# One unit's sums moved to an output bank pair, and stage 0's work re-ordered, in a convolution + gated-MLP kernel

## The chip, the cores and the metric

The kernel runs on one core of one Trainium2 chip. The metric is the device time of one execution in microseconds (us). All executions in this document are of mean granted TensorE clock 0.999 or 1.0 of full speed. A program on one core cannot be compared with a neighbouring core, so small differences rest on repeated runs.

## The reference

The input `x` has 8 sequences of 4096 tokens with 192 features. Each feature is convolved along its sequence with 7 taps (softmaxed weights, one set per head of 24 features). Then each of the 32768 tokens goes through a two-layer network:

```python
h = x @ w_in                                   # 192 -> 2048
g = h * (1.0 / (1.0 + np.exp(-beta * h)))      # beta: one number per hidden feature
return (g @ w_out).astype(np.float32)          # 2048 -> 192
```

## The kernel before

The kernel works in 32 **stages** of 1024 tokens (one chunk of 512 tokens from each half of the batch). A stage has 16 **units**; a unit is one block of 128 hidden features. In a unit, TensorE (PE) computes the *sums* `h` (6 matmuls into a `ph` bank pair of PSUM, 0.64 us), ScalarE applies the gate (1.1 us per unit), and PE issues some *output pairs*: two matmuls that add one hidden block's part of `g @ w_out` for 128 tokens (0.083 us per pair). An output **job** is 256 tokens x 16 blocks = 32 pairs, so a stage owes 4 jobs = 128 pairs. There are only two places for jobs, the bank pairs `pa` and `pb`; jobs alternate between them, and before a place can be used again VectorE must reduce it to SBUF.

```python
LAG = 2
def ready(self, s, u):                       # a job may use a block only LAG units after its sums
    fcs = NF if self.s < s else max(0, u - LAG + 1)
    return self.done < fcs * self.nb         # nb = 2: two pairs per block
...
def output(s, u, pairs, free):
    for _ in range(pairs):
        for name in free:
            if slots[name] is None and waiting:
                slots[name] = waiting.popleft()
        ...                                  # the oldest job that is ready issues one pair
        if job.po is None:
            job.po = place[name]()           # takes bank pair "a" or "b": PE waits here for its last reduce
        if job.pair():
            job.leave()                      # VectorE reduces, the DMA stores
            slots[name] = None
```

The main loop decides how many pairs each unit issues. Stage 0 issues fewer, because nothing older is waiting:

```python
first_work = {                               # VectorE, stage 0; None = next convolution tap of chunk 1
    4: [None, None],
    5: [None],
    6: [conv1_evac, lambda: scale_w_out(2), None],
    7: [None, lambda: rows_of(2)],
    8: [lambda: scale_w_out(3), None],
    9: [None],
}
QUOTA_A = {4: 2, 7: 4, 8: 4}
for s in range(N_ST):
    jobs_of(s)
    for u in range(NF):
        ...
        hidden(s, u)                         # the sums and their activation (cut: units 0 and 1, second())
        if s > 0:
            output(s, u, 8 if s < N_ST - 1 else 6, "ab")
        elif u > 8:
            output(s, u, 5 if u < NF - 1 else 10, "ab")
        elif u in QUOTA_A:
            output(s, u, QUOTA_A[u], "a")
        ...
```

So stage 0 issues 2 + 4 + 4 + 6 x 5 + 10 = 50 pairs, and every later stage but the last issues 16 x 8 = 128, as many as it owes.

`w_out` is multiplied by 1/beta in four quarters, the first two on GpSimd, the others on VectorE; `x` of chunk 1 is transposed on PE by a plain matmul with the identity, half of it into `pb` and half into `pa`.

## Time and profile before

| | before |
|---|---|
| median of 3 runs | 690.08 us (689.89 to 690.16) |
| span of the profiled run | 688.0 us |
| PE busy | 682.2 us, 99% |
| ScalarE / VectorE busy | 579.0 / 524.7 us |
| stage 1 starts (first sums) | 29.39 us |
| period from the start of stage 1 to that of stage 31 | 20.92 us |

The page's busy line (engine, busy us, share of the span, instructions) and the first line of the chain that ended last:

```profile
PE 682.2 (99%) x11312; PEld 521.1 (76%) x11312; DVE 524.7 (76%) x467; ACT 579.0 (84%) x530; POOL 9.9 (1%) x20
...
PE 98%; DMA 1%; ACT 0%; DVE 0%; issue 0%; ACTq 0%
```

PE bounds the kernel: it is nearly always busy and nearly the whole chain is its own work. The timeline of PE (start us, duration us, engine, line, operation, out<-in, count, and in brackets the idle time before it with what ended it) lists only two gaps after the start-up:

```profile
12.77 0.36 PE L368 MATMUL pa<-ident_b,x1b 64*128 64x64 bf16 x12
13.82 0.82 PE L424 MATMUL ph<-ct,w_in_s 64*128 64x512 bf16 x6 [0.70 <-ACT g L432]
14.82 0.82 PE L424 MATMUL ph<-ct,w_in_s 64*128 64x512 bf16 x6 [0.18 <-ACT g L432]
```

After the transposes, PE idles 0.70 us and then 0.18 us until ScalarE has freed a `ph` pair. The change aims at these. The timeline of VectorE in stage 0 (from the first tap of chunk 1) and GpSimd's second scaling:

```profile
15.39 1.69 DVE L338 TENSOR_SCALAR ct<-xt,cw 128x1024 bf16<-128x1024 bf16 x1
17.12 2.60 DVE L340 SCALAR_TENSOR_TENSOR ct<-xt,cw,ct 128x1024 bf16<-128x1024 bf16 x2
...
22.03 2.60 DVE L340 SCALAR_TENSOR_TENSOR ct<-xt,cw,ct 128x1024 bf16<-128x1024 bf16 x2
24.54 1.27 DVE L106 CAST xb<-xf 128x768 bf16<-128x768 f32 x2
...
25.81 0.94 DVE L314 TENSOR_TENSOR w_out_s<-w_out_raw,beta_r 128x768 bf16<-128x768 f32 x1
26.67 2.59 DVE L340 SCALAR_TENSOR_TENSOR ct<-xt,cw,ct 128x1024 bf16<-128x1024 bf16 x2
```

```profile
15.14 1.66 POOL L314 TENSOR_TENSOR w_out_s<-w_out_raw,beta_r 128x768 bf16<-128x768 f32 x1 [0.99 <-DMA w_out_raw<-in_moe_w_out_dram]
```

The first tap (15.39) took 1.69 us, as GpSimd's scaling ran until 16.80. The last w_out scaling (25.81) is done at 26.75; PE first needs that quarter at 27.50.

### The profile page before, as it was taken

The page shows a single profiled execution, that of the slowest core. Times are in us where ns is not written, and L with a number is a line of the kernel's source. Part 1 is how long each engine was busy: PE and PEld are TensorE (multiplying, and loading weights), DVE is VectorE, ACT ScalarE, POOL GpSimd, SP SyncE. Part 2 cuts the span into 40 slices and gives each one's busy share as a digit, 9 for nine tenths or more (in the row PEclk, how much of TensorE's full clock was granted, in tenths as well). Part 3 has the DMA queues.
Part 4 walks back from the last instruction along what each step waited for, and adds up shares of the span by engine and source line. Part 5 has one row for each costly group of instructions (what it writes and reads, how often), then busy time and mean ns, then how long its engine had stood idle before and what let it go on. Part 6 is the DMA issues. An engine that isn't in the chain of part 4 may idle for free.

```text
span 688.0 us, 24344 instructions
## 1 busy us (share of the span) xinstructions
PE 682.2 (99%) x11312; PEld 521.1 (76%) x11312; DVE 524.7 (76%) x467; ACT 579.0 (84%) x530; POOL 9.9 (1%) x20
## 2 busy tenths in 40 slices
PE   8999999999999999999999999999999999999998
PEld 4777777777777777777777777777777777777777
DVE  7989877788777787777797777887777977777712
ACT  7988888888888888888888888888888888888893
POOL 5000000000000000000000000000000000000000
PEclk9999999999999999999999999999999999999999
DMA  9734333244332244332444332444323443322111
GB/s 234 190 97 117 105 100 98 58 107 117 101 99 77 77 116 116 95 99 61 98 117 105 93 97 57 116 117 96 103 60 93 117 109 96 100 59 59 49 36 59
DMA packets 121861, 67.06 MB, mean 97 GB/s; under 512 B 53264, under 2 KB 121760, under 8 KB 121760
## 3 DMA queue, kind: packets, MB, share of 16 engines
q1 hardware_dynamic: 120048, 64.12, 34.7%
q0 software_dynamic: 1664, 1.38, 1.2%
q8 instruction: 88, 1.44, 0.9%
q14 instruction: 13, 0.11, 0.0%
q10 hardware_dynamic: 48, 0.01, 0.0%
HBM read 29.89 MB, written 25.17 MB: 80 GB/s over the span
## 4 chain that ended last, share of the span: by engine, by line
PE 98%; DMA 1%; ACT 0%; DVE 0%; issue 0%; ACTq 0%
PE ph L424 48%; PE pa L457 25%; PE pb L457 24%; DMA x<-in_x_dram 1%; PE pb L287 1%; ACT g L432 0%; PE ph L287 0%; DVE x0b L226 0%; ACT xt L302 0%; PE pa L287 0%; PE pb L233 0%; PE ph L233 0%; DVE diag L260 0%; ACT osb L473 0%; ACT beta L309 0%
## 5 line engine op out<-in xcount | busy, mean ns | idle before, releaser
L432 ACT ACTIVATE g<-ph,beta 128x1024 bf16<-128x1024 f32 x512 | 569.7, 1115 | 94.5 <-PE ph L424 89.8
L457 PEld LDWEIGHTS <-g 64*128 64x128 bf16 x8160 | 370.7, 94 | 102.3 <-issue 0.2
L424 PE MATMUL ph<-ct,w_in_s 64*128 64x512 bf16 x3072 | 424.3, 376 | 0.9 <-ACT g L432 0.9
L340 DVE SCALAR_TENSOR_TENSOR ct<-xt,cw,ct 128x1536 bf16<-128x1536 bf16 (+2 forms) x190 | 336.9, 1773 | 2.5
L457 PE MATMUL pa<-w_out_s,g 64*128 64x192 bf16 x4112 | 244.8, 243 | 0.0
L457 PE MATMUL pb<-w_out_s,g 64*128 64x192 bf16 (+1 forms) x4048 | 230.4, 243 | 0.0
L424 PEld LDWEIGHTS <-w_in_s 64*128 64x128 bf16 x3072 | 159.6, 94 | 54.8 <-issue 2.7
L475 DVE TENSOR_REDUCE osb<-pa 128x384 f32<-128x768 f32 x64 | 61.3, 958 | 122.5 <-PE pa L457 121.1
L475 DVE TENSOR_REDUCE osb<-pb 128x384 f32<-128x768 f32 x63 | 60.3, 957 | 29.1 <-PE pb L457 29.1
L106 DVE CAST xb<-xf 128x768 bf16<-128x768 f32 x60 | 40.5, 677 | 0.0
L338 DVE TENSOR_SCALAR ct<-xt,cw 128x1536 bf16<-128x1536 bf16 (+2 forms) x32 | 32.4, 1011 | 0.0
L473 ACT COPY osb<-pb 128x192 f32<-128x192 f32 x1 | 0.3, 319 | 7.2 <-PE pb L457 7.2
L211 POOL DMA_DIRECT2D w_in_s<-in_moe_w_in_dram x8 | 5.2, 662 | 0.0
L223 PE MATMUL ph<-zeros 128*128 128x512 bf16 (+2 forms) x11 | 4.1, 485 | 1.1 <-DVE warm L180 1.1
L287 PE MATMUL pb<-xt,diag 64*128 64x512 f32 (+1 forms) x21 | 4.7, 443 | 0.0
L121 DVE COPY xt<-xt 128x18 bf16<-128x18 bf16 x27 | 4.4, 164 | 0.0
L287 PEld LDWEIGHTS pb<-xt,diag 64*128 64x128 f32 (+1 forms) x21 | 2.7, 187 | 0.9 <-issue 0.4
L314 POOL TENSOR_TENSOR w_out_s<-w_out_raw,beta_r 128x768 bf16<-128x768 f32 x2 | 3.1, 1564 | 4.1 <-DVE beta_r L354 3.2
L223 PEld LDWEIGHTS <-zeros 128*128 128x128 bf16 x11 | 1.2, 121 | 2.2 <-issue 1.1
L181 ACT ACT_TABLE_LOAD x1 | 1.3, 1283 | 1.8 <-PEq L593 1.8
L226 ACT CAST x1b<-x 128x384 bf16<-128x384 f32 x3 | 2.0, 714 | 0.4 <-DMA x<-in_x_dram 0.4
L287 PE MATMUL ph<-xt,diag 128*128 128x512 f32 x7 | 1.9, 409 | 0.1
(55 smaller groups left out, 26.9 us busy)
## 6 DMA issues: line engine op xcount, KB each, us to landing
out_dram<-osb SPq DMA_DIRECT2D x127, 192.0 KB, 2.2
xf<-in_x_dram SPq DMA_DIRECT2D x60, 384.0 KB, 4.3
xt<-xb SPq DMA_TRANSPOSE x120, 2.6
x<-in_x_dram SPq DMA_DIRECT2D x4, 384.0 KB, 4.9
w_out_raw<-in_moe_w_out_dram SPq DMA_DIRECT2D x4, 384.0 KB, 13.5
w_in_s<-in_moe_w_in_dram POOLq DMA_DIRECT2D x6, 192.0 KB, 10.5
w_in_raw<-in_moe_w_in_dram SPq DMA_DIRECT2D x2, 192.0 KB, 5.6
w_in_s<-in_moe_w_in_dram POOLq DMA_DIRECT2D x2, 96.0 KB, 7.4
```

Source lines behind the costliest of these rows:

```text
L106: nc.vector.tensor_copy(xbs[ch][:, :, :, h, :], xfs[ch][:, h].rearrange("q b (p c) -> q b c p", c=NG),)
L121: nc.vector.tensor_copy(dst, last[:, :, HALO + TOK - PAD :])
L211: nc.gpsimd.dma_start(out=w_in_s[r * DG : (r + 1) * DG, :, c0:c1], in_=w_in_v[:, :, c0:c1])
L223: nc.tensor.matmul(pf[:, 0, 0:cols], zeros, zc, start=True, stop=True)
L287: nc.tensor.matmul(pv, diag[rows, k, :], xt[rows, o : o + TOK], start=(k == k0), stop=(k == K - 1),)
L314: (nc.vector if i > 1 else nc.gpsimd).tensor_tensor(w_out_s[:, fcs, :], w_out_raw[:, fcs, :], beta_r[:, fcs].unsqueeze(2).to_broadcast((12 ...
L338: nc.vector.tensor_scalar_mul(dst, src, scalar)
L340: nc.vector.scalar_tensor_tensor(out=dst, in0=src, scalar=scalar, in1=dst, op0=ALU.mult, op1=ALU.add)
L424: nc.tensor.matmul(ph[:, h, :], w_in_s[rows, j, fc * 128 : (fc + 1) * 128], cts[s][rows, j, :], start=(j == 0), stop=(j == NG - 1),)
L432: nc.scalar.activation(gs[s][:, fc], ph, AF.Silu, scale=beta[:, fc : fc + 1])
L457: nc.tensor.matmul(self.po[:, r, b * D : (b + 1) * D], g[rows, fc, self.h, q * BLK : (q + 1) * BLK], w_out_s[rows, fc, :], start=(self.don ...
L475: nc.vector.tensor_reduce(dst, self.po[:, :, 0 : nb * D].rearrange("p r n -> p n r"), axis=mybir.AxisListType.X, op=ALU.add,)
```

## The change

The intent: unit 2 need not wait for a `ph` pair if its sums go to the output pair `pa`, idle at that time. For this all of chunk 1's transposes must fit in `pb`, which they do as bf16 transposes. The convolution taps on PE are done in two units instead of three, a third scaling goes to GpSimd, VectorE's work is re-ordered, and the time won is used to issue 14 early output pairs (5 + 5 + 4) instead of 10.

```diff
--- before.py
+++ after.py
@@ -311,7 +311,7 @@
 
     def scale_w_out(i):
         fcs = slice(i * NQ, (i + 1) * NQ)
-        (nc.vector if i > 1 else nc.gpsimd).tensor_tensor(
+        (nc.vector if i > 2 else nc.gpsimd).tensor_tensor(
             w_out_s[:, fcs, :],
             w_out_raw[:, fcs, :],
             beta_r[:, fcs].unsqueeze(2).to_broadcast((128, NQ, D)),
@@ -352,39 +352,40 @@
     nc.vector.tensor_tensor(dst, pv, dst, ALU.add)
     cast_rows(nc.vector.tensor_copy, x1b, x1, 3)
     nc.vector.reciprocal(beta_r, beta)
-    scale_w_out(0)
-    scale_w_out(1)
+    for i in range(NW - 1):
+        scale_w_out(i)
 
 
     def second():
         xt = new_xt(1)
+        pt = in_b().bitcast(BF16)
+        for b in range(NB):
+            for c in range(NG):
+                for r in range(2):
+                    rows = slice(r * DG, (r + 1) * DG)
+                    o = ((b // 2 * NG + c) * 2 + b % 2) * DG
+                    nc.tensor.transpose(
+                        pt[:, r, o : o + DG],
+                        x1b[rows, b, c].rearrange("q h p -> q (h p)"),
+                        ident_b[rows, rows],
+                    )
         for i in range(2):
-            pt = (in_b, in_a)[i]()
-            for b in range(2):
-                for c in range(NG):
-                    for r in range(2):
-                        rows = slice(r * DG, (r + 1) * DG)
-                        o = (c * 2 + b) * DG
-                        nc.tensor.matmul(
-                            pt[:, r, o : o + DG],
-                            x1b[rows, 2 * i + b, c].rearrange("q h p -> q (h p)"),
-                            ident_b[rows, rows],
-                            start=True,
-                            stop=True,
-                        )
             t = HALO + i * 2 * BLK
+            o = i * NG * BLK
             for r in range(2):
                 nc.vector.tensor_copy(
                     xt[:, :, t + r * BLK : t + (r + 1) * BLK].rearrange(
                         "p c (q b) -> p c q b", b=2
                     ),
-                    pt[:, r, 0 : NG * BLK].rearrange("p (c b q) -> p c q b", c=NG, b=2),
+                    pt[:, r, o : o + NG * BLK].rearrange(
+                        "p (c b q) -> p c q b", c=NG, b=2
+                    ),
                 )
         halo(1, xt0)
         nc.vector.tensor_copy(xt1[:, HALO - PAD :], xt[:, 0, HALO - PAD :])
 
 
-    CONV1 = {4: (1, 3), 5: (3, 5), 6: (5, K)}
+    CONV1 = {4: (0, 5), 5: (5, K)}
     conv1_ps = []
 
     def conv1(k0, k1):
@@ -527,21 +528,18 @@
 
     first_work = {
         4: [None, None],
-        5: [None],
-        6: [conv1_evac, lambda: scale_w_out(2), None],
-        7: [None, lambda: rows_of(2)],
-        8: [lambda: scale_w_out(3), None],
-        9: [None],
+        5: [None, conv1_evac],
+        6: [None, None],
+        7: [None, None],
+        8: [lambda: rows_of(2), lambda: scale_w_out(3)],
     }
 
-    QUOTA_A = {4: 2, 7: 4, 8: 4}
+    QUOTA_A = {6: 5, 7: 5, 8: 4}
     queue = deque()
     for s in range(N_ST):
         jobs_of(s)
         for u in range(NF):
-            if s == 0 and u == min(CONV1):
-                conv1(0, 1)
-            if s > 0 or u > 1:
+            if s > 0 or u > 2:
                 hidden(s, u)
             elif u == 0:
                 phs = [hidden(0, fc, [0]) for fc in range(2)]
@@ -549,6 +547,8 @@
                     for fc in range(2):
                         hidden(0, fc, [j], phs[fc])
                 second()
+            elif u == 2:
+                hidden(0, u, ph=in_a())
             if s > 0:
                 output(s, u, 8 if s < N_ST - 1 else 6, "ab")
             elif u > 8:
```

## The prediction

> **What bounds it now.** TensorE: the page gives it 682.2 of 688.0 us busy (99%), and the chain of waits is 98% PE. Every matmul of before is still issued afterwards (same shapes, same number, 24 transposes still in one block), so only PE's idle gaps can change, and they lie in the first 30 us. The timeline of PE shows two: 0.70 us before unit 2's sums (13.82) and 0.18 us before unit 3's (14.82), both waiting for ScalarE to free a "ph" buffer. After that ScalarE paces stage 0: activations start every 1.07 us without a break, and PE, with 0.64 us of sums and 0.42 us of output pairs per unit, follows it with almost no idle.
>
> **What the change does on PE.** Unit 2's sums go to "pa" straight after the transposes, so the 0.70 us gap fills. But units 3 and 4 still wait for the activations of units 0 and 1 (ends 13.8 and 14.8), so about 0.1 + 0.35 us idle reappears, and the convolution taps of chunk 1 still wait for VectorE's xt1 (15.5, now about 15.6, since the first cast waits for all 24 transposes). I expect 0.3 us net gain there: unit 9 starts near 21.7 (before 21.56), but with 14 output pairs done instead of 10, worth 4 x 0.083 = 0.33 us.
>
> **What it does on VectorE.** A 0.95 us scaling moves to GpSimd (1.5 to 1.7 us there, off the path: its data lands near 19, needed at 23). The last quarter's scaling, however, moves from before the last two taps to behind all seven taps and the two row casts. From the timeline: tap 0 ends at 17.1 either way; it took 1.69 us because it waited for GpSimd's second scaling (15.14 to 16.80). The Trainium skill, "SBUF — State Buffer", "Who interferes with whom", says a VectorE operation in a two-port mode and a GpSimd one exclude each other; the trace agrees, as the same operation on 1536 elements takes 1.00 us later. Then taps 1-2 to 19.7, eviction to 21.1, taps 3-6 (1.29 each) to 26.3, row casts 1.27 to 27.5, last scaling 0.95 to 28.5. Before, that scaling ended at 26.75, and PE used it at 27.50 (unit 14, first output pair, the 13th block). After, PE gets there at about 27.5 to 27.8 in the same program order and must wait to about 28.55. That wait, 0.8 to 1.1 us, is on the critical path, and PE has no later idle to absorb it.
>
> **Sum.** PE's first output of unit 14 moves from 27.50 to 28.55 (+1.05) with four more pairs done (-0.33): +0.7 us. Predicted 690.8 us (before 690.08), 8 in 10 between 689.8 and 691.6. Chance of faster by over 2%: 0.005; within 2%: 0.99; slower by over 2%: 0.005.
>
> **What would show each step.** PE's timeline: no gap before unit 2's sums (start near 13.1), small gaps before units 3 and 4. VectorE's timeline: the one remaining w_out scaling at 27.5, after two casts. PE's waits: a new entry, output matmul waiting for VectorE's w_out scaling, about 1 us, once. GpSimd: a third scaling at 19 to 21. From 31 us on, the same pattern shifted by about 0.7 us. The delayed row transposes of chunk 2 (27.5 instead of 25.84) should cost PE nothing.
>
> **What would make it wrong.** If the bf16 evictions of the transposes run at double rate (0.25 us less each), tap 0 could start before GpSimd's second scaling, VectorE's chain would end 1.5 us earlier, and no wait would arise: about 689.7. If GpSimd's third scaling takes the shared port ahead of tap 2 (18.4 to 19.7; the same page says two SBUF inputs suffice, no trace here shows it), the chain grows by up to 1.5 us: about 692. If other work on PE fills the gap, less.

## More of the kernel before

Finally, the start of stage 1, with all engines (weight loads, activations and transfers left out).

```profile
30.04 0.51 PE L457 MATMUL pa<-w_out_s,g 64*128 64x192 bf16 x8
...
30.37 0.51 PE L457 MATMUL pb<-w_out_s,g 64*128 64x192 bf16 x8
30.59 0.96 DVE L475 TENSOR_REDUCE osb<-pa 128x384 f32<-128x768 f32 x1 [1.32 <-PE pa L457]
...
30.70 0.83 PE L424 MATMUL ph<-ct,w_in_s 64*128 64x512 bf16 x6
...
31.34 0.68 PE L457 MATMUL pb<-w_out_s,g 64*128 64x192 bf16 x12
...
31.84 0.35 PE L457 MATMUL pa<-w_out_s,g 64*128 64x192 bf16 x4
...
32.00 0.83 PE L424 MATMUL ph<-ct,w_in_s 64*128 64x512 bf16 x6
```

Job 0 (in `pa`) issues its last four pairs at 30.04, job 1 (in `pb`) its last ten from 30.37; VectorE reduces `pa` from 30.59 to 31.55; job 2 takes `pa` at 31.84, after the reduction was done. From one group of sums (30.70) to the next (32.00) is one unit, 1.308 us by the unrounded starts.

## The result, and the profile after

| | before | after |
|---|---|---|
| median | 690.07 us (4 runs, 689.89 to 690.16) | 693.99 us (4 runs, 693.34 to 694.83) |
| ratio | | 1.0058, 95% interval 1.004 to 1.0075 |
| span of the profiled run | 688.0 us | 691.6 us |
| stage 1 starts | 29.39 us | 30.57 us |
| period from the start of stage 1 to that of stage 31 | 20.92 us | 21.00 us |
| last unit's sums start | 674.12 us | 677.84 us |
| last output matmuls start | 683.15 us | 686.76 us |

A ratio is the mean time of one kernel's runs over that of the other's in the same rounds, so it is not quite the ratio of the medians. The loss of 3.9 us is clear of the noise.

The table splits the 3.6 us of the two profiled spans: 1.18 us are lost by the start of stage 1, 2.54 us more by the last unit (677.84 - 674.12 = 3.72), and the tail gives back 0.11. The page's two lines:

```profile
PE 685.2 (99%) x11312; PEld 520.2 (75%) x11312; DVE 521.3 (75%) x466; ACT 578.7 (84%) x530; POOL 11.3 (2%) x21
...
PE 96%; DVE 2%; DMA 1%; ACT 0%; issue 0%
```

**Stage 0.** PE's timeline around unit 2, and at unit 14:

```profile
12.70 0.53 PE L367 MATMUL pb<-ident_b,x1b 64*128 64x64 bf16 x24
13.04 0.83 PE L425 MATMUL pa<-ct,w_in_s 64*128 64x512 bf16 x6
...
14.93 0.37 PE L425 MATMUL ph<-ct,w_in_s 64*128 64x512 bf16 x1 [0.18 <-ACT g L433]
15.69 0.61 PE L425 MATMUL ph<-ct,w_in_s 64*128 64x512 bf16 x4 [0.39 <-DMA w_in_s<-in_moe_w_in_dram]
```

```profile
27.01 0.84 PE L425 MATMUL ph<-ct,w_in_s 64*128 64x512 bf16 x6
28.69 0.34 PE L458 MATMUL pa<-w_out_s,g 64*128 64x192 bf16 x4 [0.84 <-DVE w_out_s L314]
```

The 0.70 us gap is gone: the sums into `pa` start at 13.04. But unit 4's sums start one matmul at 14.93 and the next at 15.69: they wait for `w_in` data. And at unit 14 the first output pair waits until 28.69. PE's waits in the whole run (waiter <- releaser: us in total, times, longest) name both:

```profile
PE pa L458 <- DVE w_out_s L314: 0.8, 1, 0.8
PE ph L425 <- DMA w_in_s<-in_moe_w_in_dram: 0.4, 1, 0.4
```

VectorE and GpSimd show why the scaling is late:

```profile
15.67 0.48 DVE L338 TENSOR_SCALAR ct<-xt,cw 128x1024 bf16<-128x1024 bf16 x1
16.18 3.73 DVE L340 SCALAR_TENSOR_TENSOR ct<-xt,cw,ct 128x1024 bf16<-128x1024 bf16 x2
...
21.25 5.25 DVE L340 SCALAR_TENSOR_TENSOR ct<-xt,cw,ct 128x1024 bf16<-128x1024 bf16 x4
26.41 1.28 DVE L106 CAST xb<-xf 128x768 bf16<-128x768 f32 x2
...
27.68 0.96 DVE L314 TENSOR_TENSOR w_out_s<-w_out_raw,beta_r 128x768 bf16<-128x768 f32 x1
```

```profile
16.05 1.47 POOL L314 TENSOR_TENSOR w_out_s<-w_out_raw,beta_r 128x768 bf16<-128x768 f32 x1 [1.79 <-DMA w_out_raw<-in_moe_w_out_dram]
19.98 1.47 POOL L314 TENSOR_TENSOR w_out_s<-w_out_raw,beta_r 128x768 bf16<-128x768 f32 x1 [2.46 <-DMA w_out_raw<-in_moe_w_out_dram]
```

The last scaling starts at 27.68, behind all taps and the two row casts; before, it started at 25.81. In this run w_out's data landed a little later, so tap 0 (15.67, 0.48 us) ran ahead of GpSimd's second scaling (16.05). Then one of the next two taps was held up: 3.73 us for two, against 2.60 before.

**Stages 1 to 31.** The handover at the start of stage 1:

```profile
31.21 0.51 PE L458 MATMUL pa<-w_out_s,g 64*128 64x192 bf16 x8
...
31.55 0.51 PE L458 MATMUL pb<-w_out_s,g 64*128 64x192 bf16 x8
31.76 0.96 DVE L476 TENSOR_REDUCE osb<-pa 128x384 f32<-128x768 f32 x1 [3.13 <-PE pa L458]
...
31.88 0.83 PE L425 MATMUL ph<-ct,w_in_s 64*128 64x512 bf16 x6
...
32.52 0.34 PE L458 MATMUL pb<-w_out_s,g 64*128 64x192 bf16 x4
...
32.77 0.67 PE L458 MATMUL pa<-w_out_s,g 64*128 64x192 bf16 x12
...
33.27 0.83 PE L425 MATMUL ph<-ct,w_in_s 64*128 64x512 bf16 x6
```

Job 1 now has only six pairs left when job 0 is done (four at 31.55, two at 32.52). Four matmuls (two pairs) normally last 0.17 us from start to next start, but job 2 starts at 32.77, 0.25 us after 32.52. VectorE's reduction of `pa` ends at 31.76 + 0.96 = 32.72. So PE stands still for 0.08 us waiting for it. The starts of the sums (31.88 and 33.27 here) show the same in each later stage: the second unit takes 1.39 instead of 1.31 us (in the last stage, with six pairs a unit, 1.23 instead of 1.14). 31 x 0.082 = 2.54 us.

That gap is in no list of PE's waits and in no bracket of its timeline, because the modelled end of a matmul (each lasts 0.24 us here) overlaps it. The table by window of before, then after, both for 200 to 400 us (PE busy and matmuls; then weight loads, VectorE, ScalarE, GpSimd, clock, DMA share, GB/s):

```profile
200.00:400.00 200.00, 200.00 (x3368) 153.69 (x3366) 159.09 (x136) 170.37 (x154) 0.00 (x0) 1.00 0.38 99
```

```profile
200.00:400.00 200.00, 200.00 (x3352) 152.40 (x3349) 158.17 (x136) 169.82 (x153) 0.00 (x0) 1.00 0.38 99
```

PE is "200.00 of 200.00 busy" in both, but after the change it issues 16 matmuls fewer in that time, and the weight loads are busy 152.40 instead of 153.69 us. This agrees with the Trainium skill, "Perfetto Trace Analysis", "Identifying the Most-Contended Engine": matmul busy share is not a good measure of how close PE is to its limit, and weight-load busy share is one of the two measures to use instead. It shows the direction only: it fell by 0.8%, while the period grew by 0.4%.

### The profile page after: what moved, and what is told of

It is laid out like the page before. It is cut to its first block, busy times and chain, and to the rows that moved or that the text cites. A ratio compares the mean times of both kernels' runs of the same rounds, so it can differ in the third digit from the quotient of the medians.

```text
span 691.6 us, 24344 instructions
## 1 busy us (share of the span) xinstructions
PE 685.2 (99%) x11312; PEld 520.2 (75%) x11312; DVE 521.3 (75%) x466; ACT 578.7 (84%) x530; POOL 11.3 (2%) x21
## 4 chain that ended last, share of the span: by engine, by line
PE 96%; DVE 2%; DMA 1%; ACT 0%; issue 0%
PE ph L425 47%; PE pa L458 25%; PE pb L458 24%; DVE ct L340 1%; DMA x<-in_x_dram 1%; DVE xt L376 0%; PE ph L287 0%; PE pb L287 0%; DVE ct L404 0%; DVE xb L106 0%; DVE x0b L226 0%; ACT g L433 0%; DVE w_out_s L314 0%; ACT xt L302 0%; PE pa L287 0%
## 5 line engine op out<-in xcount | busy, mean ns | idle before, releaser
L458 PE MATMUL pb<-w_out_s,g 64*128 64x192 bf16 (+1 forms) x4048 | 235.4, 243 | 0.0
L376 DVE COPY xt<-pb 128x384 bf16<-128x384 bf16 x4 | 1.9, 550 | 0.6 <-PE pb L367 0.6
```

What stands on the lines that cost most here:

```text
L458: nc.tensor.matmul(self.po[:, r, b * D : (b + 1) * D], g[rows, fc, self.h, q * BLK : (q + 1) * BLK], w_out_s[rows, fc, :], start=(self.don ...
```

## The experiments

All kernels gave correct results. The theory after the result: the four extra early pairs shift the phase of the jobs, and the first two jobs of every stage then end so close together that job 2 waits for job 0's reduction (the **handover**). The rivals: the later loss comes from stage 0's VectorE or GpSimd order, which might persist as a lag; or from the new banks.

Why the phase persists: in a stage's later units, jobs 0 and 1 of that stage run side by side, and two pairs of each become ready per unit. At its end job 0 has 28 pairs, and job 1 the rest of what was issued: 50 - 28 = 22 before, 54 - 28 = 26 after. So 10 or 6 pairs of job 1 are left, of which 4 are issued next to job 0's last 4. As every stage issues just what it owes, the number repeats in each.

### 54 pairs in the kernel before

```diff
-                output(s, u, 5 if u < NF - 1 else 10, "ab")
+                output(s, u, 5 if u < NF - 1 else 14, "ab")
```

> The kernel before, with one number changed: the last unit of stage 0 issues 14 output pairs instead of 10, so 54 pairs are done before stage 1, as in the changed kernel. Handover theory (jobs 0 and 1 of a stage now end so close together that job 2 must wait for job 0's bank pair to be reduced): a gap of about 0.08 us in the second unit of each of the 31 later stages, 2.5 us, plus 0.33 us for four pairs done earlier, minus 0.1 to 0.33 us in the tail: about 692.8 us. Rival (the later loss comes from stage 0's VectorE or GpSimd order, not from the number of pairs): 690.1 us, no gaps.

Measured: 693.63 us (693.0 to 693.71) against 690.51 (median of 7); ratio 1.0036, interval 1.0016 to 1.0056. PE's timeline shows the late start of job 2 (33.12, 0.25 us after 32.87):

```profile
31.89 0.51 PE L457 MATMUL pb<-w_out_s,g 64*128 64x192 bf16 x8
...
32.87 0.35 PE L457 MATMUL pb<-w_out_s,g 64*128 64x192 bf16 x4
33.12 0.67 PE L457 MATMUL pa<-w_out_s,g 64*128 64x192 bf16 x12
```

Every later stage has one such long unit, 2.56 us in sum. One number in the old kernel, with no change of banks, scalings or VectorE order, brings the later loss; the rival expected 690.1. The total is 0.8 us above the expected 692.8. In the profiled execution stage 1 starts at 30.92, 1.2 us later than the four pairs explain (29.39 + 0.33): unit 2 already starts 0.42 us later than in the profile of before, and unit 4 waits 0.42 us for `w_in` data.

### The changed kernel with 50 pairs

```diff
-    QUOTA_A = {6: 5, 7: 5, 8: 4}
+    QUOTA_A = {6: 3, 7: 3, 8: 4}
```

> The changed kernel, with stage 0's early output pairs put back from 14 to 10 (3, 3, 4 in units 6 to 8). Handover theory: the 0.08 us gaps of the later stages vanish (-2.5 us), the wait for the last w_out scaling in unit 14 stays (it hides the four pairs taken out), the tail gives back -0.1 to +0.2: about 691.3 us against 694.0. Rival: stays at 693.5 to 694.

Measured: 691.18 us (690.66 to 691.69); ratio to before 1.0003, interval 0.9982 to 1.0023. No long units after stage 1 starts, though unit 14 still waits for the scaling (1.3 us). In the same rounds the runs of before were spread up to 693.08, which hides the rest of the difference; the absence of gaps is clear.

This run also shows what GpSimd's third scaling can do. VectorE's taps 3 to 6, then GpSimd's third scaling:

```profile
21.15 6.18 DVE L340 SCALAR_TENSOR_TENSOR ct<-xt,cw,ct 128x1024 bf16<-128x1024 bf16 x4
```

```profile
20.82 1.47 POOL L314 TENSOR_TENSOR w_out_s<-w_out_raw,beta_r 128x768 bf16<-128x768 f32 x1 [2.09 <-DMA w_out_raw<-in_moe_w_out_dram]
```

Four taps took 6.18 us; the same four took 5.25 us in the first profile after the change, in which that scaling had started at 19.98 and was nearly over (21.45) when the taps began at 21.25. Here it started at 20.82 and ran until 22.29, and the first of the taps took 2.22 us instead of 1.28.

### VectorE's order of before, 54 pairs kept

```diff
-        7: [None, None],
-        8: [lambda: rows_of(2), lambda: scale_w_out(3)],
+        7: [lambda: rows_of(2)],
+        8: [lambda: scale_w_out(3), None, None],
```

> The changed kernel with VectorE's order of before: row casts and the last w_out scaling ahead of the last two taps, 14 pairs kept. Theory: the 0.84 us wait of unit 14 goes, so does the 0.3 us of pace lost around it, the 0.08 us gaps of the later stages stay: about 692.8 us, against 694.0. Rival (the scaling wait is the source of the later gaps too): about 690.2.

Measured: 693.46 us (692.31 to 694.34), ratio 1.0035, interval 1.0012 to 1.0057. The wait for the scaling is gone from PE's waits, and the later gaps stay (2.57 us). So the gaps do not come from that wait. The total moved less than expected: in the profiled execution (694.34 us, the slowest of the four) PE waited 1.9 us for `w_in` data in units 2 to 4, 0.4 us in the first profile after the change. That this took the gain in all four is likely but not shown.

### Both edits

```diff
-    QUOTA_A = {6: 5, 7: 5, 8: 4}
+    QUOTA_A = {6: 3, 7: 3, 8: 4}
-        7: [None, None],
-        8: [lambda: rows_of(2), lambda: scale_w_out(3)],
+        7: [lambda: rows_of(2)],
+        8: [lambda: scale_w_out(3), None, None],
```

> Both of the former two edits: 10 early pairs and VectorE's order of before, leaving the bank change, the bf16 transposes and the third scaling on GpSimd. Theory: neither gap nor wait, 690.0 to 690.4 us, equal to before within 0.1%: the bank change alone gains nothing, because unit 4 waits for its w_in data and ScalarE paces the rest of stage 0. Rival (the bank change is itself worth 0.3 us or more): below 689.8.

Measured: 690.64 us (690.21 to 690.9), ratio 0.9993, interval 0.9969 to 1.0017. Neither gap nor scaling wait; equal to before within the noise. The rival, a gain from the bank change, is not seen. Together the two edits take away the whole loss.

### Dose: 52 and 56 pairs in the kernel before

```diff
-                output(s, u, 5 if u < NF - 1 else 10, "ab")
+                output(s, u, 5 if u < NF - 1 else 12, "ab")    # and, in the other, 16
```

> Dose: the kernel before with 12 pairs in the last unit of stage 0 (52 in all). Between the end of job 0 and the start of job 2 PE then has one group of sums and 8 pairs, 0.64 + 0.67 = 1.31 us, more than the 1.22 us that the handover took in the changed kernel: no gaps in the later stages, total equal to before within 0.2 us plus at most 0.17. Rival (any extra early pair costs in proportion): half of the 14-pair loss, about +1.5 us.

> Dose: 16 pairs in the last unit of stage 0 (56 in all). Job 1 then ends 4 pairs after job 0, in the same unit, and PE has only 0.64 + 0.33 = 0.98 us of other work before job 2: gaps of 1.22 - 0.98 = 0.25 us in each of 31 stages, 7.7 us, plus up to 0.5 us in stage 0: about 698 us. Rival (proportional): +4.5 us, about 694.7.

Measured: with 12, 690.07 us (689.81 to 691.41), ratio 1.0003, interval 0.9988 to 1.0018, no long units. With 16, 698.31 us (698.12 to 698.67) against 690.25, ratio 1.012, interval 1.0103 to 1.0137. The timeline of the latter at the start of stage 1 (all engines, other lines left out):

```profile
30.92 0.51 PE L457 MATMUL pa<-w_out_s,g 64*128 64x192 bf16 x8
...
31.25 0.51 PE L457 MATMUL pb<-w_out_s,g 64*128 64x192 bf16 x8
31.47 0.96 DVE L475 TENSOR_REDUCE osb<-pa 128x384 f32<-128x768 f32 x1 [1.82 <-PE pa L457]
...
32.48 0.84 PE L457 MATMUL pa<-w_out_s,g 64*128 64x192 bf16 x16
```

Both jobs end in the same unit; job 2 starts at 32.48, just after the reduction (31.47 + 0.96 = 32.43). All 31 stages have one long unit, 7.65 us in sum. The rule that fits all four doses: the handover takes 1.22 to 1.23 us from the end of job 0's issue to the start of job 2 (31.55 to 32.77 after the change, 31.25 to 32.48 here): 0.21 us until the reduction starts, 0.96 for it, 0.05 until job 2 starts. It is measured at 54 and 56 pairs; the results for 52 and 56 were expected from it before they ran. PE's other work in between is one group of sums, 0.64 us, and the rest of job 1, 0.083 us per pair:

| kernel before: pairs before stage 1 | job 1 pairs left after job 0 | PE work between | gap, 1.22 - work | median, us |
|---|---|---|---|---|
| 50 | 10 | 1.47 | none | 690.1 to 690.5 |
| 52 | 8 | 1.31 | none | 690.07 |
| 54 | 6 | 1.14 | 0.08 x 31 = 2.5 | 693.63 |
| 56 | 4 | 0.97 | 0.25 x 31 = 7.7 | 698.31 |

The loss is a threshold, not a price per pair; the proportional rival expected 694.7 for the last.

The totals also contain a start-up that differs from execution to execution. From the start of stage 1 to the last unit's sums it drops out. That stretch takes 644.7 us in the profile of before and in the profiles of the other kernels with 50 or 52 pairs (those of the bank change below among them). It takes 2.54 to 2.57 us more in the four profiles with 54 pairs and 8 pairs in each unit, whatever their banks and VectorE order, and 7.65 us more with 56 pairs. At 56 pairs a list does show the gap: weight loads for output pairs waited 32 times, 11.5 us in all, against once, 0.2 us, in before.

### 54 pairs, but more work inside the handover

On top of the changed kernel with VectorE's order of before:

```diff
-                output(s, u, 8 if s < N_ST - 1 else 6, "ab")
+                output(s, u, {0: 5, 1: 5, 2: 14}.get(u, 8) if s < N_ST - 1 else 6, "ab")
```

> The changed kernel with VectorE's order of before and all 14 early pairs kept, but with 5, 5 and 14 output pairs in units 0, 1 and 2 of stages 1 to 30 instead of 8, 8, 8, so that a second group of sums lies between the end of job 0 and the start of job 2. Handover theory: the gaps vanish in stages 1 to 30 with as many pairs done early; about 2.4 us below the same kernel without it (693.5 in the first set), 690.3 to 691.2. Rival (more early pairs cost later whatever the spacing): 693 or more.

Measured: 690.95 us (690.29 to 691.28), ratio 1.001, interval 0.9996 to 1.0025; no long unit of the 1.39 kind is left in stages 1 to 30. The timeline at the start of stage 1:

```profile
31.37 0.27 PE L458 MATMUL pb<-w_out_s,g 64*128 64x192 bf16 x2
...
31.46 0.84 PE L425 MATMUL ph<-ct,w_in_s 64*128 64x512 bf16 x6
31.60 0.96 DVE L476 TENSOR_REDUCE osb<-pa 128x384 f32<-128x768 f32 x1 [2.56 <-PE pa L458]
...
32.10 0.60 PE L458 MATMUL pb<-w_out_s,g 64*128 64x192 bf16 x10
...
32.52 0.84 PE L425 MATMUL ph<-ct,w_in_s 64*128 64x512 bf16 x6
...
33.16 1.35 PE L458 MATMUL pa<-w_out_s,g 64*128 64x192 bf16 x28
```

Job 1's last pairs are now split by a group of sums, and after another group job 2 starts at 33.16, well after the reduction (31.60 + 0.96 = 32.56). With the handover covered, the same 54 pairs cost 0.34 us from the start of stage 1 to the last unit, instead of 2.57: 0.08 in the last stage, whose pairs were not moved, and one delay of 0.26 us in stage 10, whose cause was not looked for. Rival refuted.

### The bank change alone, and a variant

The first edit: the changed kernel with the third scaling back on VectorE, VectorE's order of before and 50 pairs. The variant issues unit 4's convolution taps ahead of its sums:

```diff
-        (nc.vector if i > 2 else nc.gpsimd).tensor_tensor(
+        (nc.vector if i > 1 else nc.gpsimd).tensor_tensor(
 ... scale_w_out(0) and (1) in front, scale_w_out(2) in unit 6; QUOTA_A {6: 3, 7: 3, 8: 4}
+            if s == 0 and u == 4:           # the variant only
+                conv1(*CONV1[4])
```

> The bank change alone: unit 2's sums in the output pair, bf16 transposes in the other, convolution taps in units 4 and 5; the third w_out scaling back on VectorE, VectorE's order of before, 10 early pairs. Theory: no later gaps, no scaling wait; PE's wait moves from unit 2 to the w_in data of unit 4: equal to before within 0.5 us. If the bank change were a loss in itself: 691 or more; if a gain, below 689.8.

> The bank change alone again, with more rounds. If it costs nothing: within 0.3 us of before. If, as the first run hints (691.03 against 690.25), the sums of unit 4 now stand in PE's order ahead of the ready convolution taps and wait there for w_in data: 0.3 to 1 us slower than before.

> The same with the five convolution taps of unit 4 issued ahead of unit 4's sums instead of behind them, so that they fill the wait for w_in. If that order is what the bank change costs: equal to before within 0.3 us, and faster than the bank change alone by up to 0.8 us. Rival (it costs nothing, or it costs by waits in units 2 and 3): same time as the bank change alone.

Measured: the bank change alone 691.03 us, ratio 1.0013, interval 0.9998 to 1.0028; again with 5 rounds on another chip 690.71, ratio 1.0005, interval 0.9993 to 1.0018. The variant: 690.52, ratio 1.0009, interval 0.9995 to 1.0022. In its profiles PE's 0.70 us wait for ScalarE is gone and waits for `w_in` data stand in its place: 1.9 us in the first run, 0.9 us in the second. But the data also landed later: the fourth of GpSimd's `w_in` transfers, which unit 4 needs, at 17.59 and 16.52 us, against 15.52 in the profile of before; when it landed at 17.11, the old kernel with 54 pairs waited for it too (0.42 us). How much the bank change itself adds stays open. The variant has 0.3 us of those waits, and 0.7 us waiting for VectorE's converted rows; its total is the same as that of the bank change alone within the noise, so its theory and its rival are not told apart. No gain was seen, and a cost of 0.1% is neither shown nor excluded. No version tried is shown to be faster than the kernel before.

### The changed kernel once more

> The changed kernel itself once more, on the chip of the next two runs, for its spread. Theory: about 2.5 us of later gaps in every run; the rest of the loss varies with when the w_out and w_in data land, because GpSimd's third scaling (starting when its data lands) can hold up a VectorE tap and lengthen the wait of unit 14: 693 to 695, PE's wait for the last scaling 0.8 to 1.4 us.

Measured: 693.89 us (692.96 to 694.78), ratio 1.0052, interval 1.0038 to 1.0066. The gaps are there (2.55 us); PE's wait for the scaling is 1.3 us, with GpSimd's third scaling at 20.84 and taps 3 to 6 taking 5.83 us. In the three profiles with this VectorE order, the third scaling started at 19.98, 20.82 and 20.84, and PE waited 0.84, 1.3 and 1.3 us. This fits the landing of w_out's data as a source of the spread of 2 us, but three profiles don't prove it, and `w_in`'s landing varied too.

## Why the prediction was wrong

The prediction was 690.8 us, 689.8 to 691.6; measured 693.99.

- **"So only PE's idle gaps can change, and they lie in the first 30 us"**: the first half right, the whole loss is idle PE time; the second half wrong. 2.54 us of the loss are new gaps after 30 us, one in each of stages 1 to 31.
- **Unit 2's gap fills, small waits return**: right in size, wrong in source. PE's list gives 0.2 us for ScalarE and 0.4 us for `w_in` data; unit 9 started at 21.71 (predicted 21.7), so that agreement is partly luck. The wait for `w_in` could have been read from the trace of before: the last of unit 4's data landed at 15.52, and the change starts unit 4's sums at 14.93 instead of 15.93.
- **The last scaling ends at about 28.5 and PE waits 0.8 to 1.1 us for it**: right. It ended at 28.63, PE went on at 28.69 (predicted 28.55), and the listed wait is 0.84 us. Going back to the old order removed that wait.
- **GpSimd and VectorE block each other**: right, but "tap 0 ends at 17.1 either way" was not: it ended at 16.15, ahead of the second scaling, and tap 1 was blocked instead (2.41 us). That the chain had the same length (eviction at 19.83, before 19.73) is luck. The risk that the prediction named, GpSimd's third scaling in the way of a tap, came true in two later profiles, one tap further on (5.83 and 6.18 us for taps 3 to 6). The bf16 evictions ran at no double rate: 550 ns each, against 525 ns that the Trainium skill's `120 + FD/Accel` cycles ("VectorE: DVE Perf Modes", "The TRN2 errata") give as an estimate for 384 elements without acceleration, at 0.96 GHz.
- **The step that failed**: "with four more pairs done (-0.33)" and "From 31 us on, the same pattern shifted by about 0.7 us". Behind both stands the assumption that gaps can change only "in the first 30 us". I booked four early pairs as 0.33 us of work saved later. They were worth +2.54 us in stages 1 to 31, and only 0.11 us came back in the tail: +2.43 instead of -0.33. The runs show the mechanism: they shorten what PE has to do between two jobs below the 1.22 us of a handover, and 54 pairs in the old kernel alone bring the same loss (2.56 us). In numbers: predicted 1.05 - 0.33 = 0.72; found 1.18 + 2.54 - 0.11 = 3.61 in the profiled pair.

The needed numbers were in the trace of before: job 2 started 0.29 us after the reduction that it needs (31.84 against 31.55), and the four pairs take 4 x 0.083 = 0.33 us, more than that slack. (Where job 2 had to wait, it started 0.05 us after the reduction's end; 0.33 + 0.05 - 0.29 = 0.09 us is close to the gap of 0.08.) I looked only for idle that could absorb a delay, not for slack that the moved work was covering.

## What to carry to other kernels

Work that fills a steady loop also hides latencies in it, so before moving some of it forward into the prologue, read how much slack the double-buffered places have at their handover: the period's phase is set once and paid in every iteration. A prologue change should be checked by the period of the steady state, measured from start to start, since a gap of 80 ns under overlapping matmul records showed in no idle column here. If the period has changed, move one number (here the pairs of one unit) in the old kernel to see whether the phase alone does it.

## What the Trainium skill lacked or had wrong

- "Perfetto Trace Analysis", "Identifying the Most-Contended Engine", is borne out (weight loads 152.40 against 153.69 us in 200 us while PE is 100% busy in both), but neither it nor "Optimization Strategy" says how to find a gap that overlapping matmul records cover: here 0.082 us per stage, seen only as 1.39 us between the starts of successive groups where 1.31 is normal. Its advice to look for gaps between slices misses it in the matmul row here; only with 56 pairs, at 0.25 us, does the weight-load row list it.
- The same page, "Matmuls", says to rotate through PSUM banks so that evacuation overlaps. No page gives the size of a handover between two jobs of one bank pair: 1.22 us here, of which the reduction is 0.96 us, with a threshold (8 pairs left cost nothing, 6 pairs left 0.08 us and 4 pairs left 0.25 us each time).
- Nothing was wrong on GpSimd and VectorE: "SBUF — State Buffer", "Who interferes with whom", held, including its statement that a VectorE instruction with two SBUF inputs contends with a GpSimd one that reads SBUF: two taps took 3.73 us with a scaling beside them and 2.60 us without, and four took 6.18 against 5.25.
